# A convolution and two MLPs on one core: the weights' decode by a timetable in half positions, with its magnitude on ScalarE, raw words through GpSimd's queue, and a network's first layer a position sooner

## Chip, core and metric

The kernel runs on one core of a Trainium2 chip. Its time is device microseconds of one execution; less is better. Engines: PE = TensorE, DVE = VectorE, ACT = ScalarE, POOL = GpSimd, SP = SyncE, which here only issues DMAs. Every engine works through its own instructions in order.

## What is computed

The reference convolves `u = x * v` along the sequence with a filter that a small network makes out of position embeddings, multiplies with `x`, and sends the result through two MLPs:

```python
# x, v: (2, 12480, 128); pos_emb: (12480, 64); S = 12480
h_mlp = np.maximum(pos_emb @ w1, 0.0) @ w2
h_filt = h_mlp * np.exp(-0.01 * pos)[:, None]
u = x * v
y = irfft(rfft(u, n=2 * S) * rfft(h_filt, n=2 * S))[:, :S]
x = (x * y).reshape(24960, 128)

r = np.maximum(x @ moe_w_in, 0.0)        # w_in (128, 2048), w_out (2048, 128)
x = (r * r) @ moe_w_out
h = x @ moe2_w_in
out = (h * np.cos(h)) @ moe2_w_out
```

## The kernel before

The order of every engine's instructions is written out by hand. There are three stages.

**Stage 1** (the first `with ExitStack() as st` block) transforms the inputs over the first of two factors of the sequence length. It loops over 30 chunks of two positions each, 60 positions (`seq`). A chunk is loaded by SP into one of `LDB = 5` slots (`load`, tile `ld`; chunk q + 5 is issued when PE is done with chunk q). POOL multiplies `x` and `v` into `ut` (`times`, up to `LM = 4` positions ahead). PE makes the filter network's first layer for a whole chunk (`mlp1`, tiles `hp` and `hT`), and its second layer for a position (`prep`, tile `hp2`); ACT moves both out of PSUM. `pair` then runs four matmuls of 384 columns into `A` (in the order lists `x4`; the trace has two records for each), ACT copies a half of the results to `v`, and DVE adds and subtracts into `bt`. ACT's queue stores `bt` of a chunk to the DRAM tensor `Bs` (`store`); `bt` has `BT = 3` buffers, so a chunk's `bt` waits for the store of three chunks before.

Between positions the MLPs' weights are decoded. They come as 64-bit floats, seen as pairs of 32-bit words, and end as two float32r tensors each: `wh`, the rounded value, and `wl`, the rest. There are 16 decode steps (`WORDER`) of 128 x 512 weights. In the kernel before, `weight` is a generator with seven `yield`s per step, and `decode(2)` behind each of the positions 2 to 58 moves it on by two of them, so that a step takes 3.5 positions. SP loads the raw words (`wr`, two buffers), one step ahead.

**Stage 2** reloads `Bs` in the other order (`load2`, tile `B`), forms products with the filter's spectrum and transforms back, writing `Ds`. Its first reload waits for the store of chunk 27; `direct` and `load_late` bring the last chunks, in part straight out of `bt`.

**Stage 3** (from some 460 us on) runs the rest of the transform and both MLPs, in a fixed schedule of steps.

Of the kernel before, what the change touches and what calls it, by code (L numbers as in the profile page):

```python
# [25 lines left out]
NCH, CB = 30, 2  # L26
# [4 lines left out]
NF = DFF // 128  # L31
# [5 lines left out]
WORDER = [0, 1, 2, 3, 4, 5, 6, 7, 8, 12, 9, 13, 10, 14, 11, 15]  # L37
# [20 lines left out]
def conv_moe(ctx, tc, t):  # L58
    nc = tc.nc
# [13 lines left out]
    W = {}  # L73
# [4 lines left out]
    wt = ctx.enter_context(tc.tile_pool(name="wt", bufs=1))
    raws = {}

    def raw_of(step):
        m, f0 = divmod(step, 4)
        f = slice(4 * f0, 4 * f0 + 4)
        raw = wt.tile([128, 4, 128, 2], I32, tag="wr", name="wr", bufs=2)
        src = t[("moe_w_in", "moe_w_out", "moe2_w_in", "moe2_w_out")[m]].bitcast(I32)
        src = src.rearrange("(f p) (e t) -> p f e t" if m % 2 else "p (f e t) -> p f e t", f=NF, t=2)
        nc.sync.dma_start(out=raw, in_=src[:, f])
        raws[step] = raw, W[1 + m // 2, m % 2], f

    def weight(step):  # L90
        if step not in raws:
            raw_of(step)
        n = WORDER.index(step) + 1
        if n < 16:
            raw_of(WORDER[n])
        raw, (wh, wl), f = raws.pop(step)
        lo, hi = raw.bitcast(U32)[:, :, :, 0], raw[:, :, :, 1]
        a, b, r = (wt.tile([128, 4, 128], I32, tag=f"w_{n}", name=f"w_{n}") for n in "abr")
        af, bf, rf = a.bitcast(F32), b.bitcast(F32), r.bitcast(F32)
        ts = nc.vector.tensor_scalar  # L100
        yield
        ts(out=a, in0=hi, scalar1=0x7fffffff, scalar2=None, op0=ALU.bitwise_and)
        ts(out=b, in0=hi, scalar1=-0x80000000, scalar2=0x40000000, op0=ALU.bitwise_and, op1=ALU.bitwise_xor)
        yield
        ts(out=af, in0=af, scalar1=2.0 ** -15, scalar2=122880.0, op0=ALU.max, op1=ALU.min)
        yield
        ts(out=a, in0=a, scalar1=4, scalar2=1, op0=ALU.logical_shift_left, op1=ALU.logical_shift_right)
        nc.vector.tensor_tensor(out=a, in0=a, in1=b, op=ALU.bitwise_xor)
        yield
        ts(out=b, in0=a, scalar1=-0x800000, scalar2=None, op0=ALU.bitwise_and)  # L110
        yield
        nc.scalar.activation(wh[:, f], af, AF.Copy)
        nc.vector.scalar_tensor_tensor(out=rf, in0=lo, scalar=2.0 ** -52, in1=bf, op0=ALU.mult, op1=ALU.mult)
        yield
        nc.gpsimd.tensor_tensor(out=bf, in0=af, in1=wh[:, f].bitcast(F32), op=ALU.subtract)
        yield
        nc.gpsimd.tensor_tensor(out=wl[:, f], in0=bf, in1=rf, op=ALU.add)

    steps = (x for k in WORDER for x in weight(k))

    def decode(n):
        for _ in range(n):
            next(steps, None)
# [23 lines left out]

    with ExitStack() as st:
        out1 = st.enter_context(tc.tile_pool(name="out1", bufs=BT))
        c1 = st.enter_context(tc.tile_pool(name="c1", bufs=1))  # L150
        ring1 = st.enter_context(tc.tile_pool(name="ring1", bufs=LDB - NB, side="right"))
        io = st.enter_context(tc.tile_pool(name="io1", bufs=2))
        wk = st.enter_context(tc.tile_pool(name="wk1", bufs=2))
        psA = st.enter_context(tc.tile_pool(name="psA", bufs=3, space=PSUM))
        psM = st.enter_context(tc.tile_pool(name="psM", bufs=2, space=PSUM))

# [86 lines left out]
        def upto(kind, fn, n, end):  # L243
            while done[kind] < min(n, end):
                fn(done[kind])
                done[kind] += 1

        def last():
# [6 lines left out]
                          in_=bass.AP(t["ld"].tensor, 0, [[CB * (NCH - LATE) * 768, KE], [1, CB * (NCH - LATE) * 768]]))  # L255
        nc.scalar.dma_start(out=Gt, in_=t["G"])
        nc.scalar.dma_start(out=It, in_=t["IG"])
        for n, (q, i) in enumerate(seq):
            lead = min(LA, n + 1) if n else 1
            upto("mlp", mlp1, (n + lead - 1) // CB + 1, NCH)  # L260
            upto("times", lambda m: times(*seq[m]), n + min(LM, n + 1), len(seq))
            upto("prep", lambda m: prep(*seq[m]), n + lead, len(seq))
            pair(q, i, last if n == len(seq) - 1 else None)
            upto("mlp", mlp1, (n + lead + 1) // CB + 1 if n else 1, NCH)
            if i == 0 and q:
                if q > LATE:
                    store_late(q - 1)
                if q < NCH - 1:
                    store(q - 1)
            if (q, i) == (LATE, 0):  # L270
                load2(0)
                load2(1)
            if (q, i) == (NCH - 1, 0):
                load_late(0, CB * (NCH - 1 - LATE))
                direct(q, 0, 0)
                direct(q, 0, 1)
            if (q, i) == (NCH - 1, 1):
                load_late(1)
                load2(2)
                store(q - 1, nc.sync)  # L280
                store(q, nc.sync)
                load_late(2)
            if i == 1:
                upto("load", load, q + LDB + 1, NCH)
            if 1 < n < WS:
                decode(2)
        unread = psM.tile([128, 2 * D], F32, tag="m", name="unread")
        for _ in range(FILL[0]):
            nc.tensor.matmul(unread, w1b, w2b, start=True, stop=True)
# [515 lines left out]
```

## Time and profile before

| | |
|---|---|
| time before, median of 3 runs | 2731.67 us (2728.38 to 2733.35) |
| profiled execution, its own time | 2726.36 us |
| span of the profile (first to last instruction) | 2724.3 us |
| busy: PE, DVE, ACT, POOL | 2681.8, 2402.7, 2383.1, 1353.2 us |
| stage 1 ends (last matmul into `A`) | about 224 us |

The span is that of the profiled execution; its own time has some 2 us around it. Busy times are sums over the whole span, so they say little of stage 1, which is 8% of it; that stage is read from tables of stretches and from the rows in order of time.

### The profile page before, as it was taken

How to read it: one execution, taken by the hardware profiler on the slowest of the kernel's cores; microseconds unless marked ns; L12 is line 12 of the kernel's file. 1: busy time of each engine (PE TensorE's matmuls, PEld its weight loads, DVE VectorE, ACT ScalarE, POOL GpSimd, SP SyncE). 2: the span in 40 equal slices, each digit the busy share in tenths (PEclk: the TensorE clock that was granted, in tenths of full speed). 3: DMA queues.
4: the chain of work that ended last, by engine and by line, in shares of the span. 5: the costliest groups of instructions: out<-in, count | busy, mean ns of one | idle time of the engine just before them, and what ended most of it. 6: DMA issues, size and time to landing. Idle time of an engine off the chain costs nothing.

```text
span 2724.3 us, 38773 instructions
## 1 busy us (share of the span) xinstructions
PE 2681.8 (98%) x11762; PEld 2104.9 (77%) x11762; DVE 2402.7 (88%) x4675; ACT 2383.1 (87%) x4295; POOL 1353.2 (50%) x1050
## 2 busy tenths in 40 slices
PE   8998999999999999999999999999999999999999
PEld 5554444888888888888888888888888888888887
DVE  6997998888888888888888888888888888888888
ACT  4446997899999999999999999999999999999998
POOL 4565886244444444444444444444444444444455
PEclk9999999999999999999999999999999999999999
DMA  9997997110100110101110101111101111101000
GB/s 396 421 411 260 298 300 232 46 29 31 30 26 23 32 29 18 43 16 33 29 33 16 45 16 33 29 32 29 32 17 33 29 33 29 32 17 32 17 9 10
DMA packets 86771, 219.64 MB, mean 81 GB/s; under 512 B 6025, under 2 KB 49633, under 8 KB 82689
## 3 DMA queue, kind: packets, MB, share of 16 engines
q1 hardware_dynamic: 79298, 180.24, 20.1%
q10 hardware_dynamic: 7263, 36.92, 3.3%
q8 instruction: 93, 1.52, 0.2%
q14 instruction: 117, 0.96, 0.1%
HBM read 140.37 MB, written 77.07 MB: 80 GB/s over the span
## 4 chain that ended last, share of the span: by engine, by line
PE 81%; ACT 1%; DVE 1%; issue 0%; SPq 0%; POOLq 0%; POOL 0%; DMA 0%; DVEq 0%; ACTq 0%
PE h L565 13%; PE h L567 13%; PE y L581 13%; PE h L566 13%; PE y L579 13%; PE y L580 13%; PE pc L531 4%; DVE g L653 0%; ACT k L630 0%; DVE r L638 0%; ACT r L604 0%; DVE gh L663 0%; ACT g L610 0%; ACT c L645 0%; ACT gh L661 0%
## 5 line engine op out<-in xcount | busy, mean ns | idle before, releaser
L670 POOL TENSOR_TENSOR gl<-g,gh 128x512 fp32r<-128x512 f32 (+2 forms) x800 | 1040.8, 1301 | 1220.1 <-ACT gh L661 717.4
L653 DVE TENSOR_TENSOR g<-h,c 128x512 f32<-128x512 f32 (+2 forms) x800 | 538.6, 673 | 208.5 <-ACT c L645 197.4
L630 ACT ACTIVATE k<-h,quarter 128x512 int32<-128x512 f32 (+2 forms) x800 | 540.7, 676 | 121.5 <-PE h L567 117.4
L565 PE MATMUL h<-zh,wh 128*128 128x512 f32 (+2 forms) x1600 | 624.9, 391 | 1.2 <-DVE zh L549 0.9
L581 PE MATMUL y<-gl,wh 128*128 128x512 f32 (+2 forms) x1600 | 617.8, 386 | 4.1 <-POOL gl L670 2.2
L579 PE MATMUL y<-gh,wl 128*128 128x512 f32 (+2 forms) x1600 | 616.2, 385 | 0.7 <-DVE gh L617 0.7
L567 PE MATMUL h<-zh,wl 128*128 128x512 f32 (+2 forms) x1600 | 615.2, 384 | 0.0
L566 PE MATMUL h<-zl,wh 128*128 128x512 f32 (+2 forms) x1600 | 614.3, 384 | 0.0
L580 PE MATMUL y<-gh,wh 128*128 128x512 f32 (+2 forms) x1600 | 614.1, 384 | 0.0
L645 ACT ACTIVATE c<-r,halfpi 128x512 f32<-128x512 f32 (+2 forms) x800 | 565.4, 707 | 2.6 <-DVE r L638 2.6
L624 DVE TENSOR_TENSOR gl<-g,gh 128x512 fp32r<-128x512 f32 (+2 forms) x800 | 535.8, 670 | 1.1
L638 DVE CUSTOM_DVE_ANT_0 r<-h,k 128x512 f32<-128x512 f32 (+2 forms) x800 | 535.6, 669 | 0.0
L604 ACT ACTIVATE r<-h 128x512 f32<-128x512 f32 (+2 forms) x800 | 471.5, 589 | 69.2 <-PE h L567 57.0
L610 ACT ACTIVATE g<-r 128x512 f32<-128x512 f32 (+2 forms) x800 | 492.9, 616 | 1.0 <-DVE gl L624 0.4
L617 DVE CAST gh<-g 128x512 fp32r<-128x512 f32 (+2 forms) x800 | 331.9, 415 | 37.8 <-ACT g L610 34.9
L581 PEld LDWEIGHTS y<-gl,wh 128*128 128x128 f32 x1600 | 300.3, 188 | 70.3 <-POOL gl L670 7.7
L579 PEld LDWEIGHTS y<-gh,wl 128*128 128x128 f32 x1600 | 300.4, 188 | 61.2 <-DVE zl L592 1.2
L580 PEld LDWEIGHTS y<-gh,wh 128*128 128x128 f32 x1600 | 300.7, 188 | 59.6
L567 PEld LDWEIGHTS h<-zh,wl 128*128 128x128 f32 x1600 | 300.4, 188 | 59.7
L565 PEld LDWEIGHTS h<-zh,wh 128*128 128x128 f32 x1600 | 300.9, 188 | 56.9 <-issue 1.0
L566 PEld LDWEIGHTS h<-zl,wh 128*128 128x128 f32 x1600 | 300.7, 188 | 54.9
L661 ACT ACTIVATE gh<-g 128x512 fp32r<-128x512 f32 (+2 forms) x400 | 246.0, 615 | 0.1
(67 smaller groups left out, 2426.2 us busy)
## 6 DMA issues: line engine op xcount, KB each, us to landing
ld<-ld SPq DMA_DIRECT2D x30, 1336.0 KB
B<-Bs SPq DMA_DIRECT2D x25, 1536.0 KB
dt<-Ds SPq DMA_DIRECT2D x59, 416.0 KB
Ds<-dt SPq DMA_DIRECT2D x24, 960.0 KB
Bs<-bt ACTq DMA_DIRECT2D x28, 768.0 KB
Bs<-bt ACTq DMA_DIRECT2D x28, 480.0 KB
xt<-xT SPq DMA_DIRECT2D x60, 208.0 KB
out<-o SPq DMA_DIRECT2D x47, 256.0 KB
```

The source lines that it names most:

```text
L565: nc.tensor.matmul(h[:, :n], wh[:, f, :], zh[:, :n], start=True, stop=False)
L566: nc.tensor.matmul(h[:, :n], wh[:, f, :], zl[:, :n], start=False, stop=False)
L567: nc.tensor.matmul(h[:, :n], wl[:, f, :], zh[:, :n], start=False, stop=True)
L579: nc.tensor.matmul(y[:, :n], wl[:, f, :], gh[:, :n], start=a, stop=False)
L580: nc.tensor.matmul(y[:, :n], wh[:, f, :], gh[:, :n], start=False, stop=False)
L581: nc.tensor.matmul(y[:, :n], wh[:, f, :], gl[:, :n], start=False, stop=b)
L624: nc.vector.tensor_tensor(out=gl[:, :n], in0=g[:, :n], in1=gh[:, :n].bitcast(F32), op=ALU.subtract)
L630: nc.scalar.activation(k[:, :n], hp[2, u][:, :n], AF.Identity, scale=-1.0, bias=quarter)
L638: nc.vector._custom_dve(TENSOR_ADD_SAT, out=r[:, :n], in0=h[:, :n], in1=k[:, :n], s0=0.25, s1=-0.75)
L645: nc.scalar.activation(c[:, :n], r[:, :n], AF.Sin, bias=halfpi, scale=TWO_PI)
L653: nc.vector.tensor_tensor(out=g[:, :n], in0=h[:, :n], in1=c[:, :n], op=ALU.mult)
L670: nc.gpsimd.tensor_tensor(out=gl[:, :n], in0=g[:, :n], in1=gh[:, :n].bitcast(F32), op=ALU.subtract)
```

## The change

The decode becomes a timetable. Step k starts at half position 8 + 20 k / 3 (whole part), so a step comes every 10/3 positions, and each of its parts has a place in half positions behind that start: 0 `open_` (ACT), 2 `clamp`, 3 `shift`, 5 `exponent` and 6 `low` (DVE), 6 `high` (ACT), 9 `rest` and 10 `both` (POOL). At 8 the raw words of step k + 3 are loaded. `decode(n)` runs behind every position n and does what is planned for half positions 2n and 2n + 1.

The magnitude of the high word is taken by an ACT instruction (Abs with a scale) where two DVE instructions took magnitude and sign apart; the sign is merged back in by one instruction with two tensors, and the exponent is written over the raw word. DVE has five instructions a step instead of seven. The raw words get three buffers instead of two and are loaded through GpSimd's queue, not SP's. The decode's tiles move into stage 1's own memory. From position 9 on, `mlp1` is called a position sooner.

```diff
-WS = 59
+RAWS, PART0 = 3, 8
...
-        raw = wt.tile([128, 4, 128, 2], I32, tag="wr", name="wr", bufs=2)
-        nc.sync.dma_start(out=raw, in_=src[:, f])
-    def weight(step):
-        raw, (wh, wl), f = raws.pop(step)
-        lo, hi = raw.bitcast(U32)[:, :, :, 0], raw[:, :, :, 1]
-        yield
-        ts(out=a, in0=hi, scalar1=0x7fffffff, scalar2=None, op0=ALU.bitwise_and)
-        ts(out=b, in0=hi, scalar1=-0x80000000, scalar2=0x40000000, op0=ALU.bitwise_and, op1=ALU.bitwise_xor)
-        yield
-        ts(out=af, in0=af, scalar1=2.0 ** -15, scalar2=122880.0, op0=ALU.max, op1=ALU.min)
-        yield
-        ts(out=a, in0=a, scalar1=4, scalar2=1, op0=ALU.logical_shift_left, op1=ALU.logical_shift_right)
-        nc.vector.tensor_tensor(out=a, in0=a, in1=b, op=ALU.bitwise_xor)
-        yield
-        ts(out=b, in0=a, scalar1=-0x800000, scalar2=None, op0=ALU.bitwise_and)
-        yield
-        nc.scalar.activation(wh[:, f], af, AF.Copy)
-        nc.vector.scalar_tensor_tensor(out=rf, in0=lo, scalar=2.0 ** -52, in1=bf, op0=ALU.mult, op1=ALU.mult)
-        yield
-        nc.gpsimd.tensor_tensor(out=bf, in0=af, in1=wh[:, f].bitcast(F32), op=ALU.subtract)
-        yield
-        nc.gpsimd.tensor_tensor(out=wl[:, f], in0=bf, in1=rf, op=ALU.add)
...
+            raw = wt.tile([128, 4, 128, 2], I32, tag="wr", name="wr", bufs=RAWS)
+            nc.gpsimd.dma_start(out=raw, in_=src[:, f])
...
+        def weight(k):
+            at, step = PART0 + k * 20 // 3, WORDER[k]
+            def open_():
+                nc.scalar.activation(a[0].bitcast(F32), hold[0].bitcast(F32)[:, :, :, 1], AF.Abs, scale=2.0 ** 16)
+            def clamp():
+                nc.vector.tensor_scalar(out=af, in0=af, scalar1=2.0, scalar2=1.875 * 2.0 ** 32, op0=ALU.max, op1=ALU.min)
+            def shift():
+                nc.vector.tensor_scalar(out=a[0], in0=a[0], scalar1=3, scalar2=None, op0=ALU.logical_shift_left)
+                nc.vector.scalar_tensor_tensor(out=a[0], in0=hold[0][:, :, :, 1], scalar=-0x80000000, in1=a[0],
+                                               op0=ALU.bitwise_and, op1=ALU.bitwise_or)
+            def exponent():
+                nc.vector.tensor_scalar(out=hold[0][:, :, :, 1], in0=a[0], scalar1=-0x800000, scalar2=None, op0=ALU.bitwise_and)
+            def high():
+                nc.scalar.activation(hold[1][0][:, hold[2]], a[0].bitcast(F32), AF.Copy)
+            def low():
+                nc.vector.scalar_tensor_tensor(out=r[0], in0=raw.bitcast(U32)[:, :, :, 0], scalar=2.0 ** -52,
+                                               in1=raw.bitcast(F32)[:, :, :, 1], op0=ALU.mult, op1=ALU.mult)
+            def rest():
+                nc.gpsimd.tensor_tensor(out=af, in0=af, in1=hold[1][0][:, hold[2]].bitcast(F32), op=ALU.subtract)
+            def both():
+                nc.gpsimd.tensor_tensor(out=hold[1][1][:, hold[2]], in0=a[0].bitcast(F32), in1=r[0], op=ALU.add)
+            for d, fn in ((0, open_), (2, clamp), (3, shift), (5, exponent), (6, low), (6, high), (9, rest), (10, both)):
+                plan(d, fn)
+            if k + RAWS < len(WORDER):
+                plan(8, lambda: raw_of(WORDER[k + RAWS]))
...
+        def decode(n):
+            if n == 1:
+                for k in range(RAWS):
+                    raw_of(WORDER[k])
+            for h in (2 * n, 2 * n + 1):
+                for fn in planned.pop(h, ()):
+                    fn()
...
-            upto("mlp", mlp1, (n + lead + 1) // CB + 1 if n else 1, NCH)
+            upto("mlp", mlp1, (n + lead + 1 + (n > 8)) // CB + 1 if n else 1, NCH)
...
-            if 1 < n < WS:
-                decode(2)
+            decode(n)
```

In the order of instructions this shows at three places. First DVE, early in stage 1; `bt x2` are the two of one position, `w_a`, `w_b` and `w_r` the decode's tiles, `wr` the raw words. Before, one step:

```order
L102 TENSOR_SCALAR w_a<-wr 128x512
L103 TENSOR_SCALAR w_b<-wr 128x512
L216 TENSOR_TENSOR bt<-A,v 128x2x384 x2
L105 TENSOR_SCALAR w_a<-w_a 128x512
L107 TENSOR_SCALAR w_a<-w_a 128x512
L108 TENSOR_TENSOR w_a<-w_a,w_b 128x512
L216 TENSOR_TENSOR bt<-A,v 128x2x384 x2
L110 TENSOR_SCALAR w_b<-w_a 128x512
L113 SCALAR_TENSOR_TENSOR w_r<-wr,w_b 128x512
```

and of the change:

```order
L135 TENSOR_SCALAR w_a<-w_a 128x512
L138 TENSOR_SCALAR w_a<-w_a 128x512
L139 SCALAR_TENSOR_TENSOR w_a<-wr,w_a 128x512
L239 TENSOR_TENSOR bt<-A,v 128x2x384 x2
L143 TENSOR_SCALAR wr<-w_a 128x512
L239 TENSOR_TENSOR bt<-A,v 128x2x384 x2
L151 SCALAR_TENSOR_TENSOR w_r<-wr 128x512
```

Two instructions on the raw words left DVE, and what remains stands between the same `bt` pairs.

Second POOL, where a decode step's last two parts stand among the products `ut`. Before:

```order
L191 TENSOR_TENSOR ut<-ld 104x2x256 x3
L115 TENSOR_TENSOR w_b<-w_a,wh_67 128x512
L191 TENSOR_TENSOR ut<-ld 104x2x256
L117 TENSOR_TENSOR wl_68<-w_b,w_r 128x512
L191 TENSOR_TENSOR ut<-ld 104x2x256 x3
```

and of the change:

```order
L115 DMA wr<-moe_w_out 128x4x256
L156 TENSOR_TENSOR w_a<-w_a,wh_67 128x512
L214 TENSOR_TENSOR ut<-ld 104x2x256
L159 TENSOR_TENSOR wl_68<-w_a,w_r 128x512
L214 TENSOR_TENSOR ut<-ld 104x2x256 x2
```

A DMA issue for the raw words now stands ahead of each step's `rest` on POOL; on SP, where they stood between the loads of chunks, there are none left.

Third PE, at the ninth and tenth position; `hp` out of `ld` is the network's first layer for a chunk, `hp` out of `hT` its second for a position, `A x4` a position's matmuls. Before:

```order
L182 MATMUL hp<-ld,first 128x208
L196 MATMUL hp_373<-first,hT 104x256
L212 MATMUL A<-ut,ld 128x384 x4
L196 MATMUL hp_395<-first,hT 104x256
L212 MATMUL A<-ut,ld 128x384 x4
L182 MATMUL hp<-ld,first 128x208
L196 MATMUL hp_419<-first,hT 104x256
L212 MATMUL A<-ut,ld 128x384 x4
```

and of the change:

```order
L205 MATMUL hp<-ld,first 128x208
L219 MATMUL hp_359<-first,hT 104x256
L235 MATMUL A<-ut,ld 128x384 x4
L205 MATMUL hp<-ld,first 128x208
L219 MATMUL hp_387<-first,hT 104x256
L235 MATMUL A<-ut,ld 128x384 x4
L219 MATMUL hp_408<-first,hT 104x256
L235 MATMUL A<-ut,ld 128x384 x4
```

From here on the first layer stands ahead of a chunk's second position instead of the next chunk's first.

## Rows read from the trace of the kernel before

**Rows 1.** The page: DMA busy share in 40 slices of the span.

```profile
DMA  9997997110100110101110101111101111101000
```

**Rows 2.** Stretches A:B and length in us; busy us by engine (instructions); clock; DMA share; GB/s.

```profile
10.00:20.00 10.00, 9.06 (x21) 4.69 (x20) 1.82 (x2) 3.10 (x9) 5.19 (x5) 1.00 1.01 414
40.00:200.00 160.00, 149.64 (x503) 91.28 (x502) 156.83 (x182) 77.13 (x173) 89.99 (x70) 1.00 1.02 418
200.00:218.00 18.00, 15.97 (x54) 9.66 (x53) 17.40 (x24) 8.37 (x19) 9.64 (x8) 1.00 0.67 243
```

**Rows 3.** Groups by shape, 10 to 224 us: busy us, mean ns | idle before.

```profile
L216 DVE TENSOR_TENSOR bt<-A,v 128x768 f32<-128x768 f32 x118 | 107.1, 948 | 24.3 <-PE A L212 21.8 <-ACT v L214 1.5 <-issue 0.8
...
L102 DVE TENSOR_SCALAR w_a<-wr 128x512 int32<-128x512 int32 x16 | 23.1, 1442 | 0.5 <-DMA wr<-moe_w_in 0.5
L103 DVE TENSOR_SCALAR w_b<-wr 128x512 int32<-128x512 int32 x16 | 21.7, 1358 | 0.0
...
L105 DVE TENSOR_SCALAR w_a<-w_a 128x512 f32<-128x512 f32 x16 | 17.1, 1067 | 0.0
...
L108 DVE TENSOR_TENSOR w_a<-w_a,w_b 128x512 int32<-128x512 int32 x16 | 11.1, 692 | 0.6
L113 DVE SCALAR_TENSOR_TENSOR w_r<-wr,w_b 128x512 f32<-128x512 uint32 x16 | 11.0, 687 | 0.3
L112 ACT ACTIVATE wh<-w_a 128x512 fp32r<-128x512 f32 x16 | 10.1, 631 | 36.4 <-DVE w_a L108 36.4
...
L110 DVE TENSOR_SCALAR w_b<-w_a 128x512 int32<-128x512 int32 x16 | 6.7, 422 | 0.3
L107 DVE TENSOR_SCALAR w_a<-w_a 128x512 int32<-128x512 int32 x16 | 6.7, 419 | 0.3
```

**Rows 4.** DVE in order of time: start, us, what it is, count.

```profile
52.43 1.81 DVE L216 TENSOR_TENSOR bt<-A,v 128x768 f32<-128x768 f32 x2
```

**Rows 5.** DMA issues, 0 to 230 us: queue, count, KB (1024 bytes) each.

```profile
ld<-ld SPq DMA_DIRECT2D x30, 1336.0 KB
Bs<-bt ACTq DMA_DIRECT2D x28, 768.0 KB
Bs<-bt ACTq DMA_DIRECT2D x28, 480.0 KB
...
wr<-moe_w_in SPq DMA_DIRECT2D x8, 512.0 KB
```

**Rows 6.** PE in order of time: first A of chunks 1, 5, 26, 29; last A.

```profile
21.81 2.75 PE L212 MATMUL A<-ut,ld 104*128 104x384 f32 x8
...
47.34 2.75 PE L212 MATMUL A<-ut,ld 104*128 104x384 f32 x8
...
196.04 2.82 PE L212 MATMUL A<-ut,ld 104*128 104x384 f32 x8 [0.17 <-DVE bt L216]
...
217.42 4.88 PE L212 MATMUL A<-ut,ld 104*128 104x384 f32 x14
223.07 0.91 PE L212 MATMUL A<-ut,ld 104*128 104x384 f32 x2 [0.77 <-DVE bt L216]
```

**Rows 7.** Waits, 10 to 224 us: us in total, times, longest us.

```profile
PE A L212 <- DVE bt L216: 6.2, 11, 1.3
...
POOL ut L191 <- DMA ld<-ld: 2.5, 2, 1.4
...
DVE w_a L102 <- DMA wr<-moe_w_in: 0.5, 1, 0.5
```

**Rows 8.** Line L103 in stage 1: duration in ns, min/median/max.

```profile
L103 DVE TENSOR_SCALAR w_b<-wr x16: 415/1490/1500, 27.3 to 212.9; 128x512 int32<-128x512 int32 x16
```

**Rows 9.** SP's issues in order of time, 160 to 232 us.

```profile
188.78 0.33 SPq L165 DMA_DIRECT2D ld<-ld  x1
...
217.07 1.29 SPq L137 DMA_DIRECT2D B<-Bs  x2
```

**Rows 10.** DMA queues, 196 to 200 us, SP's (q1): packets, MB, share of engines.

```profile
q1 hardware_dynamic: 230, 0.50, 33.0%
```

More of the change, by code (lines that the diff above doesn't have):

```diff
@@ L76, in conv_moe @@
             W[layer, k] = tuple(cst.tile([128, NF, 128], F32R, name=f"w{p}{layer}{k}") for p in "hl")
[L78 to L83, printed above, removed]
-        raw = wt.tile([128, 4, 128, 2], I32, tag="wr", name="wr", bufs=2)
-        src = t[("moe_w_in", "moe_w_out", "moe2_w_in", "moe2_w_out")[m]].bitcast(I32)
-        src = src.rearrange("(f p) (e t) -> p f e t" if m % 2 else "p (f e t) -> p f e t", f=NF, t=2)
-        nc.sync.dma_start(out=raw, in_=src[:, f])
-        raws[step] = raw, W[1 + m // 2, m % 2], f
-    def weight(step):
[L91 to L95, printed above, removed]
-        raw, (wh, wl), f = raws.pop(step)
-        lo, hi = raw.bitcast(U32)[:, :, :, 0], raw[:, :, :, 1]
-        a, b, r = (wt.tile([128, 4, 128], I32, tag=f"w_{n}", name=f"w_{n}") for n in "abr")
-        af, bf, rf = a.bitcast(F32), b.bitcast(F32), r.bitcast(F32)
-        ts = nc.vector.tensor_scalar
-        yield
-        ts(out=a, in0=hi, scalar1=0x7fffffff, scalar2=None, op0=ALU.bitwise_and)
-        ts(out=b, in0=hi, scalar1=-0x80000000, scalar2=0x40000000, op0=ALU.bitwise_and, op1=ALU.bitwise_xor)
-        yield
-        ts(out=af, in0=af, scalar1=2.0 ** -15, scalar2=122880.0, op0=ALU.max, op1=ALU.min)
-        yield
-        ts(out=a, in0=a, scalar1=4, scalar2=1, op0=ALU.logical_shift_left, op1=ALU.logical_shift_right)
-        nc.vector.tensor_tensor(out=a, in0=a, in1=b, op=ALU.bitwise_xor)
-        yield
-        ts(out=b, in0=a, scalar1=-0x800000, scalar2=None, op0=ALU.bitwise_and)
-        yield
-        nc.scalar.activation(wh[:, f], af, AF.Copy)
-        nc.vector.scalar_tensor_tensor(out=rf, in0=lo, scalar=2.0 ** -52, in1=bf, op0=ALU.mult, op1=ALU.mult)
-        yield
-        nc.gpsimd.tensor_tensor(out=bf, in0=af, in1=wh[:, f].bitcast(F32), op=ALU.subtract)
-        yield
-        nc.gpsimd.tensor_tensor(out=wl[:, f], in0=bf, in1=rf, op=ALU.add)
[L119 to L123, printed above, removed]
     conv_st = ExitStack()
@@ L149, in conv_moe @@
         out1 = st.enter_context(tc.tile_pool(name="out1", bufs=BT))
+        wt = st.enter_context(tc.tile_pool(name="wt", bufs=1))
         c1 = st.enter_context(tc.tile_pool(name="c1", bufs=1))
@@ L153, in conv_moe, with raw_of @@
         wk = st.enter_context(tc.tile_pool(name="wk1", bufs=2))
+        raws = {}
+        def raw_of(step):
+            m, f0 = divmod(step, 4)
+            f = slice(4 * f0, 4 * f0 + 4)
+            raw = wt.tile([128, 4, 128, 2], I32, tag="wr", name="wr", bufs=RAWS)
+            src = t[("moe_w_in", "moe_w_out", "moe2_w_in", "moe2_w_out")[m]].bitcast(I32)
+            src = src.rearrange("(f p) (e t) -> p f e t" if m % 2 else "p (f e t) -> p f e t", f=NF, t=2)
+            nc.gpsimd.dma_start(out=raw, in_=src[:, f])
+            raws[step] = raw, W[1 + m // 2, m % 2], f
@@ new lines, in conv_moe, with plan @@
+        planned = {}
+        def weight(k):
+            at, step = PART0 + k * 20 // 3, WORDER[k]
+            a, r, hold = [], [], []
+            def plan(d, *fns):
+                planned.setdefault(at + d, []).extend(fns)
+            def open_():
+                hold.extend(raws.pop(step))
+                a.append(wt.tile([128, 4, 128], I32, tag="w_a", name="w_a", bufs=2))
+                nc.scalar.activation(a[0].bitcast(F32), hold[0].bitcast(F32)[:, :, :, 1], AF.Abs, scale=2.0 ** 16)
+            def clamp():
+                af = a[0].bitcast(F32)
+                nc.vector.tensor_scalar(out=af, in0=af, scalar1=2.0, scalar2=1.875 * 2.0 ** 32, op0=ALU.max, op1=ALU.min)
[8 more added lines that the diff above has]
+            def low():
+                raw = hold[0]
+                r.append(wt.tile([128, 4, 128], F32, tag="w_r", name="w_r"))
+                nc.vector.scalar_tensor_tensor(out=r[0], in0=raw.bitcast(U32)[:, :, :, 0], scalar=2.0 ** -52,
+                                               in1=raw.bitcast(F32)[:, :, :, 1], op0=ALU.mult, op1=ALU.mult)
+            def rest():
+                af = a[0].bitcast(F32)
+                nc.gpsimd.tensor_tensor(out=af, in0=af, in1=hold[1][0][:, hold[2]].bitcast(F32), op=ALU.subtract)
[5 more added lines that the diff above has]
+                plan(8, lambda: raw_of(WORDER[k + RAWS]))
@@ L154, in conv_moe @@
+        for k in range(len(WORDER)):
+            weight(k)
+        def decode(n):
[5 more added lines that the diff above has]
+                    fn()
         psA = st.enter_context(tc.tile_pool(name="psA", bufs=3, space=PSUM))
```

## Prediction

> **What bounds the kernel now.** I read the page first: of its 40 DMA slices (68 us each) only the first seven are busy, to 477 us [rows 1]. Behind them lies a dense stream of matmuls that this change doesn't touch. The edited code runs in stage 1, the first 224 us, and a microsecond gained there is one at the end as long as the two stages behind it merely start sooner.
>
> So next the table of stretches. From 40 to 200 us DVE is busy 156.83 us of 160, which looks like the bound. But the same row has a DMA share of 1.02 at 418 GB/s, and between 10 and 20 us, when five loads stand queued and little else runs, the share is 1.01 at 414 GB/s [rows 2]: 418 is all that these transfers get. Two resources are full at once. What each allows per chunk (two positions) can be worked out.
>
> DVE: a decode step takes 1442 + 1358 + 1067 + 419 + 692 + 422 + 687 = 6087 ns [rows 3], and comes every 3.5 positions (seven yields, two per position), which is 3.48 us per chunk. The two bt instructions of a position take 1.81 us back to back [rows 4], a little under twice their mean of 948 ns [rows 3], since they overlap; two positions add 3.62. Sum 7.10 us.
>
> Transfers: a chunk loads 1336 KB and stores 768 + 480 KB; a decode step loads 512 KB per 1.75 chunks, 293 KB [rows 5]. 2877 KB are 2.946 MB, at 418 GB/s **7.05 us**.
>
> PE: before the first decode instructions reach DVE, four chunks go from 21.81 to 47.34 us, **6.38 us** each. After that 24 chunks go from 47.34 to 217.42, 7.09 each [rows 6]. So the pace is DVE's 7.10, with the transfers' 7.05 right under it, and PE's 6.38 far below. That nearly equal second floor is what this prediction turns on.
>
> The list of waits agrees: PE's wait for DVE before A is 6.2 us in all, and nothing waits long for a load (POOL 2.5 us, DVE 0.5 us) [rows 7]. The buffers hide the transfers as long as they keep pace.
>
> **The change, part by part.**
>
> *DVE.* Five instructions take the place of seven. The sign, shift and mask parts have near twins in the old step: clamp as L105 (1067), shift as L107 (419), the two-tensor OR as L108 (692), exponent as L110 (422), low as L113 (687): 3287 ns [rows 3]. Sixteen steps fall from 97.4 to 52.6 us, **44.8 us off DVE**. Bounds: a single-source instruction takes 415 ns alone and 1.5 us when it meets a POOL instruction [rows 8], so the step lies between 2.6 us (none held up) and 5.9 (all three held up). I take 3.3, since the old order's shift and exponent met no POOL work while its first three did. With a step every 10/3 positions DVE then needs 3.62 + 3.29 × 2 / 3.33 = 5.6 us per chunk. At the upper bound it would be 7.2, and nothing would be won.
>
> *ACT.* Abs is 16 more instructions, taken as the old Copy, 631 ns [rows 3]: 10.1 us. ACT is busy for 77 of 160 us [rows 2], so idle time holds it. In exchange the Copy no longer sits at ACT's head waiting for DVE's XOR. If that cover were gone it would cost those 10 us.
>
> *POOL and SP.* Sixteen raw loads leave SP's queue, where an issue costs 0.33 us [rows 9]. SP only waits between loads, so this frees nothing: the load of chunk q+5 is issued when PE is done with chunk q. On POOL an issue isn't in the trace. From below it is SP's 0.33 us; from above POOL, busy for 90 of 160 us [rows 2], has 70 us idle, over 4 us per issue. Inside that it is hidden, the more so as times runs four positions ahead. Behind a late issue stand rest, both and the next times on POOL. The transferred bytes are the same, so the transfer floor stays; with a step every 1.67 chunks it is 7.08 us.
>
> *The first layer a position sooner.* PE's first-layer matmul for chunk c stood before the first position of chunk c − 1; it now stands before the second one of chunk c − 2. The work is the same; ACT's hT gets more room, but PE, which runs in order, wants the load a position (3.2 us) earlier.
>
> **The sum.** DVE's floor falls to 5.6, PE's is 6.38, so the transfers at 7.05 to 7.08 set the pace as long as loads arrive. Up to 200 us next to nothing can be gained: PE may creep nearer to the loads, not outrun them. What is left is the tail. The last load is issued at 188.78 us [rows 9]; SP's queue moves only 0.50 MB from 196 to 200 us [rows 10], part of it raw words, so the load has landed at about 200. From then until 218 us the DMA share is 0.67 [rows 2], and the stage ends at 223.98 (223.07 + 0.91) [rows 6].
>
> Lower bound: PE is no nearer to the loads than now. Chunk 26 starts at 196.04; four chunks at 6.38 end at 221.6, **2.4 us sooner**. Upper bound: all idle transfer time of the tail is used, 18 × (1 − 0.67 / 1.02) = **6.2 us**, after which the first reload of Bs (issued at 217.07 now [rows 9]) can't come sooner still. The new order sets a limit close to that: after the last hp five positions of 3.19 us remain, so with the load at 200 to 202 the end lies at 216.5 to 218.5. Against the upper end speaks that the last raw load, 512 KB or 1.25 us, moves from the idle tail into the full stretch (three steps are now fetched ahead), and that each chunk that PE draws nearer to the loads puts a store (1.28 MB, 3.1 us) ahead of the last load. I take the middle, **4 us**. Stage 2 starts on the reload, the last stores and the last bt, which all move along.
>
> The profiled execution took 2726.36 us (span 2724.3 and 2.1 around it) and would take 2722.4; the median of the runs shown is 2731.67, 5.3 higher, so I predict 2731.7 − 4 = **2727.7 us**. A measurement of this kernel can tell about 0.2%, 5.5 us, from no change; 4 us is inside that.
>
> **Rivals.**
>
> *Tail and rate both give, 5.5 to 9 us.* The full 6.2 us come back, or a fuller queue moves 1% more in 160 us (1.6 us). That the share of 1.02 lies over the 1.01 of the early queue speaks for it, that the two rates are within 1% of each other against. About 2724.5.
>
> *PE's pace.* If the transfers followed, 24 chunks would save 0.71 us each, 17 us: 2714.7. It needs 2.96 MB in 6.38 us, 464 GB/s, 11% over anything in [rows 2].
>
> *Hidden altogether.* What the tail gains is lost again on the way into stage 2, or DVE's instructions are held up by POOL more than I take. 2731.
>
> *Slower: raw words late through POOL.* ACT's Abs now takes the wait for them, in order, with v and so bt and PE's A buffers behind it. The load for step k+3 is issued at half position 8 of step k and read at 20: six positions, 19 to 21 us, against a step time of 3.5 × 3.54 = 12.4 us within which it arrives today nearly always (0.5 us of waits [rows 7]). It decides once POOL's issue plus landing takes over 19 us; each microsecond beyond costs up to 16: 2731.7 − 4 + 16 = 2743.7. What speaks for it: DVE and POOL do lock each other out, 415 ns against 1.5 us in [rows 8]. The Trainium skill (SBUF — State Buffer, "SBUF: two separate sides") goes further: descriptors of a DMA from GpSimd's queue are written by GpSimd, which a two-port DVE instruction keeps from the port, so such a transfer seems blocked, and it advises SP's or ACT's queue. By that rule a raw load would be held for some 0.4 us at each of three such instructions per step, 1.3 us, far from the 7 us of slack, so the sum would stay; no run here shows a DMA from POOL yet.
>
> **Chances.** The transfer floor with 2.4 to 5.4 us: 0.50. Tail and rate: 0.22. PE's pace: 0.08. Hidden: 0.11. Slower: 0.09. Faster by over 0.2% is the second and third, 0.30; within, the first and fourth, 0.61; slower 0.09. The range leaves out PE's pace and the slower case: 2722 to 2734.
>
> **What would show it.** In the changed profile: DVE's busy time from 40 to 200 us near 120 to 130 us; five decode instructions of 3.3 us in sum; DMA share still 1.0 up to some 200 us at about 418 GB/s, and no lower GB/s for the raw words; PE waiting for loads (hp or ut after ld) or DVE's bt waiting for stores, which it doesn't now; a tail of 6.4 us per chunk; the first reload of Bs at about 213. Wrong would be: a pace under 7.0 us before 200 us (then 418 GB/s is no floor), POOL's DMA rows of over 4 us, or ACT idle before Abs on the raw words.

## The result, and the profile after

The changed kernel takes 2748.83 us (median of 6 runs, 2743.54 to 2751.42), the kernel before 2732.49 (6 runs beside it): ratio 1.006, 95% interval 1.0047 to 1.0073. The change costs 16.3 us, where 4 us of gain were predicted. The profiled execution of the changed kernel took 2751.42 us, the slowest of its six, that of the kernel before 2726.36; so the traces are compared by stage 1, not by their spans.

TensorE (PE) in order of time, the changed kernel: first A of chunks 5 and 29, last A.

```profile
46.54 2.75 PE L235 MATMUL A<-ut,ld 104*128 104x384 f32 x8
...
236.99 4.88 PE L235 MATMUL A<-ut,ld 104*128 104x384 f32 x14
242.63 0.91 PE L235 MATMUL A<-ut,ld 104*128 104x384 f32 x2 [0.76 <-DVE bt L239]
```

24 chunks take 190.45 us, 7.94 each, where they took 7.09 [rows 6]. The stage ends at 243.54 us instead of 223.98: 19.6 us of loss in the stage that was edited. The two spans differ by 25.3 us; the other 5.7 us are no more than executions of one kernel lie apart (2728.38 to 2735.28 before). The decode step, instructions by line and form, 0 to 260 us (busy us, mean ns, then idle time before):

```profile
L135 DVE TENSOR_SCALAR w_a<-w_a 128x512 f32<-128x512 f32 x16 | 46.9, 2931 | 0.0
L139 DVE SCALAR_TENSOR_TENSOR w_a<-wr,w_a 128x512 int32<-128x512 int32 x16 | 14.9, 929 | 0.6
L151 DVE SCALAR_TENSOR_TENSOR w_r<-wr 128x512 f32<-128x512 uint32 x16 | 10.9, 682 | 0.5
L138 DVE TENSOR_SCALAR w_a<-w_a 128x512 int32<-128x512 int32 x16 | 10.5, 659 | 0.4
L143 DVE TENSOR_SCALAR wr<-w_a 128x512 int32<-128x512 int32 x16 | 6.7, 416 | 0.0
L115 POOL DMA_DIRECT2D wr<-moe_w_out x8 | 6.4, 802 | 45.0 <-DVE w_r L151 45.0
L115 POOL DMA_DIRECT2D wr<-moe_w_in x8 | 4.7, 591 | 31.0 <-DVE w_r L151 31.0
```

Exponent and low (L143, L151) are as sized. The clamp (L135) takes 2931 ns instead of 1067 [rows 3], and that is a mean over two kinds: its shortest takes 418 ns, its longest 5443. GpSimd (POOL) stands 76 us at the raw loads (45.0 + 31.0), waiting for low. One of these places in order of time:

```profile
82.54 0.79 POOL L115 DMA_DIRECT2D wr<-moe_w_out  x1 [5.24 <-DVE w_r L151]
83.35 1.28 POOL L156 TENSOR_TENSOR w_a<-w_a,wh 128x512 f32<-128x512 f32 x1
84.57 1.28 POOL L214 TENSOR_TENSOR ut<-ld 104x512 f32<-104x512 f32 x1
85.80 1.27 POOL L159 TENSOR_TENSOR wl<-w_a,w_r 128x512 fp32r<-128x512 f32 x1
86.07 3.73 DVE L135 TENSOR_SCALAR w_a<-w_a 128x512 f32<-128x512 f32 x1
87.02 2.49 POOL L214 TENSOR_TENSOR ut<-ld 104x512 f32<-104x512 f32 x2
...
90.91 1.82 DVE L239 TENSOR_TENSOR bt<-A,v 128x768 f32<-128x768 f32 x2
...
94.89 0.63 ACT L146 ACTIVATE wh<-w_a 128x512 fp32r<-128x512 f32 x1 [3.53 <-DVE bt L239]
...
96.68 4.51 PE L235 MATMUL A<-ut,ld 104*128 104x384 f32 x8 [1.91 <-ACT ut L221]
```

GpSimd waits 5.24 us, issues the load and then runs five instructions without a pause, to 89.51. The clamp starts in the midst of them and ends at 89.80. Nine of the sixteen clamps meet such a run, and each ends 0.28 to 0.30 us behind its last instruction. Behind it come a late bt, a late Copy on ACT (which waited 3.53 us for DVE), the ut copies behind that, and a PE that idles 1.91 us. Its next eight matmuls take 4.51 us instead of 2.75. The windows say why, 80 to 84 us behind an earlier stop, 96 to 100 behind this one (us; busy time and count of PE, PEld, DVE, ACT, POOL; granted clock; DMA share; GB/s):

```profile
80.00:84.00 4.00, 4.00 (x8) 2.08 (x8) 2.24 (x3) 0.81 (x1) 1.44 (x2) 0.59 1.02 419
...
96.00:100.00 4.00, 3.32 (x6) 1.92 (x7) 2.69 (x3) 2.41 (x7) 3.98 (x4) 0.62 0.87 339
...
40.00:200.00 160.00, 141.93 (x444) 85.56 (x443) 141.31 (x141) 76.90 (x169) 89.67 (x76) 0.94 0.99 376
200.00:220.00 20.00, 17.47 (x49) 10.00 (x48) 16.86 (x17) 7.88 (x17) 11.64 (x10) 0.83 0.84 338
```

In each microsecond from 97 to 100 the granted clock is 0.50, the lower of PE's two levels (1.2 of 2.4 GHz); before, it was 1.00 all through [rows 2]. Of the seven longest stops from 40 us on (1.57 to 2.79 us) five were followed by such a fall; the longest was not:

```profile
64.48 2.82 PE L235 MATMUL A<-ut,ld 104*128 104x384 f32 x8 [2.79 <-DVE bt L239]
...
79.72 4.51 PE L235 MATMUL A<-ut,ld 104*128 104x384 f32 x8 [1.87 <-ACT ut L221]
```

What the clock costs and what the waits cost can be told apart by PE's matmuls into A, the same 472 in both kernels (busy us, mean ns, then idle time before; first before, then after):

```profile
L212 PE MATMUL A<-ut,ld 104*128 104x384 f32 x472 | 166.8, 496 | 9.9 <-DVE bt L216 6.2 <-ACT v L214 2.9 <-ACT ut L198 0.8
```

```profile
L235 PE MATMUL A<-ut,ld 104*128 104x384 f32 x472 | 177.5, 520 | 22.2 <-DVE bt L239 13.2 <-ACT ut L221 6.8 <-issue 1.3
```

The same matmuls take 10.7 us longer, and PE stands still 12.3 us longer before them; before its second-layer matmuls it stands still 4.1 us less. With all its matmuls counted, PE is busy 157.69 us of the 170.08 from chunk 5 to 29 before, and 169.85 of 190.45 after: 12.2 us by the clock (0.93 in the mean of this stretch, instead of 1.00) and 8.2 us by waits, together the 20.4 us by which this stretch grew. The DMA share is still 0.99, but only 376 GB/s move, and past the start of the stage hardly anything waits for a transfer (DVE's bt 2.1 us in all).

### The profile page after: what moved, and what is told of

It reads as the page before. It is cut to its first block, busy times and chain, and to the rows that moved or that the text cites. A ratio compares the mean times of both kernels' runs of the same rounds, so it can differ in the third digit from the quotient of the medians.

```text
span 2749.6 us, 38811 instructions
## 1 busy us (share of the span) xinstructions
PE 2695.7 (98%) x11762; PEld 2112.3 (77%) x11762; DVE 2399.0 (87%) x4643; ACT 2391.3 (87%) x4311; POOL 1360.8 (49%) x1066
## 4 chain that ended last, share of the span: by engine, by line
PE 80%; ACT 1%; DVE 1%; DMA 0%; issue 0%; SPq 0%; POOLq 0%; DVEq 0%
PE h L587 13%; PE h L589 13%; PE h L588 13%; PE y L603 13%; PE y L601 13%; PE y L602 13%; PE pc L553 4%; DVE g L675 0%; ACT k L652 0%; DVE r L660 0%; DMA dt<-Ds 0%; ACT c L667 0%; DVE gh L685 0%; DMA Ds<-dt 0%; ACT r L626 0%
```

## The experiments

The first theory (held up): GpSimd's wait makes a run of instructions, the run holds the clamp, PE stops, its clock falls. Rivals: transfers from GpSimd's queue are slower (2.946 MB at 370 GB/s is just the pace seen), or the sooner first layer costs. Each ratio is to the kernel before, measured beside the run; its medians lie between 2730.64 and 2732.49 us, so times of different experiments can be set against each other to some 2 us only.

**1. Raw loads on SP again.**

```diff
-            nc.gpsimd.dma_start(out=raw, in_=src[:, f])
+            nc.sync.dma_start(out=raw, in_=src[:, f])
```

> Edit: the changed kernel with the raw loads issued by SP again, the rest as changed. Held-up theory (GpSimd stands at the raw load's head until low has read the buffer, then runs its queued work without a pause, DVE's clamp is held for all of it, bt comes late, TensorE idles and its granted clock falls): GpSimd waits for low no more, clamp falls from a mean of 2.9 us to 1.0-2.0, the granted clock of stage 1 stays over 0.95, time 2728 to 2738 us. Queue theory (transfers issued by GpSimd move slower, 2.946 MB at some 370 GB/s is 7.96 us a chunk, which is the pace seen): back to 418 GB/s and 7.05 us a chunk, 2728 us. First-layer theory (the sooner matmul is to blame): stays at 2749.

2735.02 us, ratio 1.001 (1.000 to 1.002); clamp 837 ns, still less than foretold. 13 us of the 16 are in this line. The held-up theory's range holds; the queue theory foretold 2728, 7 us less.

**2. First layer as before.**

```diff
-            upto("mlp", mlp1, (n + lead + 1 + (n > 8)) // CB + 1 if n else 1, NCH)
+            upto("mlp", mlp1, (n + lead + 1) // CB + 1 if n else 1, NCH)
```

> Edit: the changed kernel with the network's first layer at its old place, the rest as changed. Held-up and queue theories: 2746 to 2752 us, clamp still 2.9 us, the granted clock still falls to 0.5-0.7 in places. First-layer theory: 2728 to 2735 us.

2746.79, 1.0057 (1.0046 to 1.0069); clamp 3128 ns. The first layer is not what the 16 us are; the 2 us between 2748.83 and 2746.79 can't be told from nothing here.

**3. Raw load later on GpSimd's queue.**

```diff
-                plan(8, lambda: raw_of(WORDER[k + RAWS]))
+                plan(12, lambda: raw_of(WORDER[k + RAWS]))
```

> Edit: the changed kernel with each raw load planned at half position 12 of its step instead of 8, still on GpSimd's queue and four positions ahead of its use. Held-up theory: low is done by then, so GpSimd's wait for it falls from 76 us in all to under 15, the bursts get shorter, clamp falls below 2 us, 2730 to 2741 us. Queue theory: the rate stays at some 370 GB/s and the pace at 7.9 us a chunk, 2746 to 2752 us. First-layer theory: 2746 to 2752.

2736.44, 1.0021 (1.0012 to 1.003). GpSimd doesn't wait at the load any more, clamp 1375 ns, and from 40 to 120 us all queues together move 416 to 423 GB/s (403 and 356 in the changed kernel), with the raw words still on GpSimd's queue. The queue theory, which wanted 2746 to 2752 us, falls.

**4. Clamp with two tensor sources.**

```diff
-                nc.vector.tensor_scalar(out=af, in0=af, scalar1=2.0, scalar2=1.875 * 2.0 ** 32, op0=ALU.max, op1=ALU.min)
+                nc.vector.scalar_tensor_tensor(out=af, in0=af, scalar=2.0, in1=lim[:, None, :].to_broadcast([128, 4, 128]),
+                                               op0=ALU.max, op1=ALU.min)
```

> Edit: the changed kernel with the clamp written with two tensor sources (its upper limit from a small constant tile) instead of one, the same arithmetic. The two-source instructions of the step were held up little (0.68 and 0.93 us). Held-up theory: clamp takes 0.7 to 1.0 us instead of 2.9 although GpSimd still waits for low and still runs in bursts, bt is no longer late, granted clock over 0.95, 2728 to 2738 us. Queue theory: the pace stays at 7.9 us a chunk, 2746 to 2752. First-layer theory: 2746 to 2752.

2750.36, 1.0072 (1.006 to 1.0084); the clamp takes 3379 ns. My premise was wrong: an instruction with two sources in SBUF is held just as long, up to 5.7 us. The two-source instructions of the step had not met such a run; they were not immune to it. Against the held-up theory itself this says nothing.

**5. The wait alone** (same place and queue; only the step that is loaded differs).

```diff
-            if k + RAWS < len(WORDER):
-                plan(8, lambda: raw_of(WORDER[k + RAWS]))
+            if k and k + RAWS - 1 < len(WORDER):
+                plan(8, lambda: raw_of(WORDER[k + RAWS - 1]))
```

> Edit: the changed kernel with the raw load at the same place of GpSimd's queue (half position 8 of step k), but for step k+2 instead of k+3, into the buffer whose last reader, low of step k-1, is long done. So only GpSimd's wait goes; order, queue and bytes stay. Held-up theory: the wait of 76 us in all falls under 10, clamp falls below 2 us on average, the time falls by 9 to 15 us to 2734 to 2740. If the later place in the queue was what helped when the load stood at half position 12, nothing comes: 2746 to 2752 us.

2736.73, 1.0022 (1.0012 to 1.0031). GpSimd's wait at the load is gone, clamp 826 ns: 10 to 12 us of the 16 (10 by the ratios).

**6. Both: SP, and later.**

```diff
-            nc.gpsimd.dma_start(out=raw, in_=src[:, f])
+            nc.sync.dma_start(out=raw, in_=src[:, f])
...
-                plan(8, lambda: raw_of(WORDER[k + RAWS]))
+                plan(12, lambda: raw_of(WORDER[k + RAWS]))
```

> Edit: the changed kernel with the raw loads issued by SP and planned at half position 12, so that neither GpSimd nor SP waits for low ahead of other work. Floor theory (with the held-up DVE gone the transfers at 418 GB/s set the pace of 7.05 us a chunk, and a tail of some 4 us is won, as predicted): 2724 to 2730 us, granted clock 1.0. Clock theory (a stage that waits on transfers leaves TensorE idle for some us now and then, its granted clock falls, and that gives the gain back): 2731 to 2737 us, with stretches at 0.6 to 0.95 in stage 1.

2736.06, 1.0019 (1.0011 to 1.0028), with a granted clock of 0.94 from 40 to 200 us: no gain as the floor theory wanted it; the clock theory's range holds. ACT's Abs now waits 12.5 us for raw words.

**7 and 8. The two small parts, alone, in the kernel before**: its raw loads through GpSimd (line as in 1, the other way), and its first layer sooner (as in 2, the other way).

> Edit: the kernel before with its raw loads issued through GpSimd's queue, nothing else. There the load for the next step is asked for when a step begins, into the buffer of the step before, whose reader is done. Held-up theory: GpSimd waits little at it, 2729 to 2736 us. Queue theory (transfers issued by GpSimd are slower or slow the others): 2740 to 2752 us.

> Edit: the kernel before with the network's first layer a position sooner, nothing else. Held-up theory: no change that can be told, 2728 to 2735 us. If the sooner first layer costs by itself (TensorE, in order, wants a load a position earlier): 2736 to 2742 us.

The sooner first layer: 2733.06, 1.0007 (0.9998 to 1.0016), nothing that can be told. The raw loads through GpSimd alone: **2754.20, 1.0088 (1.0074 to 1.0102)**, more than the whole change, although GpSimd never waits at them. That contradicts the first theory, which needed the wait; the queue theory, refuted by experiment 3, comes nearer with its 2740 to 2752. Its order of time:

```profile
79.56 0.80 POOL L87 DMA_DIRECT2D wr<-moe_w_out  x1
80.38 3.72 POOL L191 TENSOR_TENSOR ut<-ld 104x512 f32<-104x512 f32 x3
...
79.83 4.56 DVE L103 TENSOR_SCALAR w_b<-wr 128x512 int32<-128x512 int32 x1
```

In the kernel before, the same three ut products let this DVE instruction in after at most one of them (1.50 us [rows 8]). Here a DMA stands ahead of them, and it waits for all three; so do six others of the sixteen (4.36 to 4.58 us). So a second theory (port): a DMA that GpSimd issues keeps DVE out until GpSimd's run ends; the wait in the changed kernel only makes the run long. (The port is an inference; the runs show how long DVE is held.) Two runs set it against the first.

**9. The wait and the run, without the DMA in it.**

```diff
-            nc.gpsimd.dma_start(out=raw, in_=src[:, f])
+            nc.sync.dma_start(out=raw, in_=src[:, f])
...
-            if k + RAWS < len(WORDER):
-                plan(8, lambda: raw_of(WORDER[k + RAWS]))
+            plan(8, lambda: nc.gpsimd.tensor_copy(seen, r[0][:, 0, 0:1]))
+            if k + RAWS < len(WORDER):
+                plan(12, lambda: raw_of(WORDER[k + RAWS]))
```

> Edit: the changed kernel with the raw loads on SP (asked for at half position 12), and in their old place on GpSimd's queue a copy of one column of low's result, 128 numbers. So GpSimd still waits for low in that place and then runs its queued work without a pause, but no DMA of its own stands in that run. Port theory (a DMA that GpSimd issues keeps DVE's instructions on SBUF out until GpSimd's run of instructions ends; without one DVE gets in after at most one of them): clamp is 1.7 us at most and 0.7 to 1.1 on average, 2732 to 2740 us. Run theory (any run of GpSimd's behind a wait holds DVE to its end): clamp up to 4 or 5 us, over 2.3 on average, 2745 to 2752 us.

2734.71, 1.0015 (1.0005 to 1.0025). GpSimd still waits 77.0 us for low and still runs on without a pause, but DVE gets in:

```profile
54.63 0.19 POOL L164 COPY seen<-w_r 128x1 f32<-128x1 f32 x1 [5.01 <-DVE w_r L152]
54.77 1.27 POOL L157 TENSOR_TENSOR w_a<-w_a,wh 128x512 f32<-128x512 f32 x1
56.00 1.28 POOL L216 TENSOR_TENSOR ut<-ld 104x512 f32<-104x512 f32 x1
57.24 1.27 POOL L160 TENSOR_TENSOR wl<-w_a,w_r 128x512 fp32r<-128x512 f32 x1
58.47 2.69 POOL L216 TENSOR_TENSOR ut<-ld 104x512 f32<-104x512 f32 x2
...
57.00 1.79 DVE L136 TENSOR_SCALAR w_a<-w_a 128x512 f32<-128x512 f32 x1
```

The clamp of 57.00 sits through the rest of one GpSimd instruction and the whole of the next and ends at 58.79, with two more of the run still to come (to 61.16). Its mean is 1076 ns, as foretold; its longest, 1.88 us, is over the 1.7 that the port theory allowed. Five fences follow, one line's instructions in each (count, then ns as min/median/max): the clamp of the changed kernel and of experiment 9, then the second mask instruction of the kernel before with raw loads through GpSimd and of experiment 10, and last the first mask instruction of the kernel before.

```profile
L135 DVE TENSOR_SCALAR w_a<-w_a x16: 418/3807/5443, 35.0 to 232.5; 128x512 f32<-128x512 f32 x16
```

```profile
L136 DVE TENSOR_SCALAR w_a<-w_a x16: 415/1104/1877, 35.7 to 217.8; 128x512 f32<-128x512 f32 x16
```

```profile
L103 DVE TENSOR_SCALAR w_b<-wr x16: 408/422/4576, 26.5 to 239.3; 128x512 int32<-128x512 int32 x16
```

```profile
L102 DVE TENSOR_SCALAR w_b<-wr x16: 415/1489/1496, 26.1 to 218.9; 128x512 int32<-128x512 int32 x16
```

```profile
L102 DVE TENSOR_SCALAR w_a<-wr x16: 417/1043/2536, 27.0 to 212.6; 128x512 int32<-128x512 int32 x16
```

The last shows that one GpSimd instruction is not the most without a DMA. In the kernel before, the first mask instruction takes 2.53 to 2.54 us seven times: the rest of a ut product and the whole of the wl behind it. That is the longest hold there, and experiment 10 keeps it (2.54); the holds to the end of a longer run are the DMA's.

The changed kernel has a test of this of its own. Four of its runs have the DMA at their head but then a pause of 0.07 to 0.08 us, here between 71.89 and 71.97:

```profile
70.61 1.28 POOL L156 TENSOR_TENSOR w_a<-w_a,wh 128x512 f32<-128x512 f32 x1
71.97 1.28 POOL L159 TENSOR_TENSOR wl<-w_a,w_r 128x512 fp32r<-128x512 f32 x1
73.20 4.10 POOL L214 TENSOR_TENSOR ut<-ld 104x512 f32<-104x512 f32 x3
73.60 1.16 DVE L135 TENSOR_SCALAR w_a<-w_a 128x512 f32<-128x512 f32 x1
```

The clamps behind the pause take 0.52 to 1.16 us, although three more GpSimd instructions follow.

**10. The kernel before, raw loads through GpSimd, but at the end of its run** (a third buffer; the pool moves into stage 1).

```diff
-        nc.sync.dma_start(out=raw, in_=src[:, f])
+        nc.gpsimd.dma_start(out=raw, in_=src[:, f])
...
-        if n < 16:
-            raw_of(WORDER[n])
+        if n == 1:
+            raw_of(WORDER[1])
...
         yield
+        if n + 1 < 16:
+            raw_of(WORDER[n + 1])
         nc.gpsimd.tensor_tensor(out=bf, in0=af, in1=wh[:, f].bitcast(F32), op=ALU.subtract)
```

> Edit: the kernel before with its raw loads through GpSimd's queue, but asked for right ahead of rest, which waits for low (a third buffer, so that no load waits). There the DMA is the last of a run of GpSimd's and an idle time follows; in the run with the raw loads on GpSimd at the start of a step it stood at the head of one. Port theory: the second mask instruction is 1.7 us at most again (4.58 there), 2729 to 2737 us. Queue theory (transfers issued by GpSimd cost by themselves): 2748 to 2756 us.

2734.23, 1.0013 (1.0003 to 1.0023): with the same queue and the same bytes 20 us come back, and the second mask instruction's longest is 1496 ns. The port theory holds in both, but for its bound of one instruction; run and queue theory fall.

**11 and 12. What do the transfers bound?** Raw loads left out but for the first buffers, in experiment 6's kernel and in the kernel before:

```diff
+            if len(kept) == RAWS:
+                raws[step] = kept[WORDER.index(step) % RAWS], W[1 + m // 2, m % 2], f
+                return
             raw = wt.tile([128, 4, 128, 2], I32, tag="wr", name="wr", bufs=RAWS)
+            kept.append(raw)
```

> Edit: the changed kernel with raw loads on SP, but only the first three of sixteen; the other thirteen steps decode what stands in the three buffers, so the weights are not the real ones; all else is done. Transfers fall from 2.94 to 2.64 MB a chunk, 6.3 us at 418 GB/s, and DVE needs 5.6 to 6.0. Floor theory (transfers bound the stage once DVE is relieved): the pace falls to TensorE's 6.4 us a chunk, 2712 to 2719 us. If something else holds the stage (order, hand-over between engines, clock): 2728 us or more.

> Edit: the kernel before, but only the first two of sixteen raw loads; the other steps decode what stands in the two buffers, so the weights are not the real ones; all else is done. By the prediction's two floors (DVE 7.10 us a chunk, transfers 7.05) DVE's stays: 2727 to 2733 us. If the transfers had set the pace before: 2712 to 2722 us.

2724.99, 0.9976 (0.9964 to 0.9989), and 2729.39, 1.000 (0.999 to 1.0009). Windows of the two:

```profile
40.00:200.00 160.00, 153.09 (x514) 94.81 (x513) 135.59 (x161) 86.52 (x190) 100.42 (x75) 0.99 0.99 388
```

```profile
40.00:200.00 160.00, 148.73 (x498) 90.23 (x497) 155.79 (x181) 75.68 (x171) 90.01 (x70) 1.00 0.98 372
```

The kernel before loses nothing and gains nothing with a tenth fewer bytes: DVE set its pace. Its DMA share stays 0.98 although only 372 GB/s move, so a share near 1 doesn't say that the transfers are full. And with both DVE and the transfers relieved, the mended kernel stands 5.7 us under the kernel before, not the 17 of PE's pace: 6.86 us a chunk instead of 6.38, and a time between the two ranges that were foretold.

Against experiment 6, which has the raw loads and is otherwise the same, it is 11 us faster, and stage 1 ends at 217.90 us instead of 232.72. So once DVE is relieved the raw words' transfers do cost, by their bytes or by when they come; these runs don't part the two.

**13 and 14. Where the last microseconds went.** To experiment 5's kernel: work for DVE that nobody reads, and the first layer as before.

```diff
+                if not between and q > 4:
+                    nc.vector.tensor_tensor(out=v[:, 0], in0=A[0][:, 0, 0:384], in1=v[:, 0], op=ALU.add)
```

> Edit: the kernel of the run in which only GpSimd's wait was taken away, and on DVE after each position's two bt instructions (from chunk 5 on) one more of half their width, whose result nobody reads. It reads PSUM and v, and takes about 0.55 us by the rows of that form. DVE then needs some 6.9 us a chunk instead of 5.8. Pacing theory (a stage that can run ahead of its transfers runs until its buffers are used up, stops for some us at a time, and TensorE's granted clock falls at each stop; a DVE just slower than the transfers' 7.05 us spreads the stops out): fewer stretches under a granted clock of 1.0, and 2729 to 2734 us, faster than the 2736.7 without the added work. Work theory (added work on a busy engine only costs): 2737 to 2745 us.

> Edit: the kernel of the run in which only GpSimd's wait was taken away, with the network's first layer at its old place as well; of the parts of the change that the runs so far put a cost on, none is left but the relieved DVE itself. First-layer part costs something: 2730 to 2734 us. Costs nothing: 2735 to 2738 us.

2739.40, 1.0025 (1.0016 to 1.0034), and 2734.69, 1.0014 (1.0006 to 1.0023). The added work brings nothing: the pacing theory isn't borne out. It isn't cleanly tested either, since the added instruction reads A, and PE waits 15.0 us (9 times) for it. The first layer's place costs at most the 2 us between 2736.73 and 2734.69, inside the spread of the runs; 2734.69 lies between the two ranges that were foretold.

What the mended kernels show instead of a gain, experiment 5 in order of time:

```profile
80.87 1.82 DVE L239 TENSOR_TENSOR bt<-A,v 128x768 f32<-128x768 f32 x2 [4.19 <-DMA Bs<-bt]
82.84 4.51 PE L235 MATMUL A<-ut,ld 104*128 104x384 f32 x8 [2.92 <-DVE bt L239]
...
222.91 4.88 PE L235 MATMUL A<-ut,ld 104*128 104x384 f32 x14
```

its waits (us in total, times, longest) and its windows:

```profile
DVE bt L239 <- DMA Bs<-bt: 24.1, 10, 4.3
```

```profile
40.00:80.00 40.00, 38.97 (x133) 24.15 (x132) 32.82 (x38) 23.22 (x52) 29.29 (x24) 1.00 1.01 422
80.00:120.00 40.00, 35.02 (x108) 21.72 (x109) 27.83 (x36) 18.31 (x41) 22.49 (x19) 0.91 1.01 401
```

and experiment 9, in which ACT's Abs stands at a raw word that SP brought late, with v behind it:

```profile
79.03 0.67 ACT L132 ACTIVATE w_a<-wr 128x512 f32<-128x512 f32 x1 [4.67 <-DMA wr<-moe_w_out]
...
80.78 4.44 PE L237 MATMUL A<-ut,ld 104*128 104x384 f32 x8
```

PE runs at its own pace until the three bt buffers are all on their way out (or a raw word is late), stops for 2 to 3 us, and in both places shown then gets a lower clock: 4.4 to 4.5 us for a group of 2.75. (At 197.24 us of experiment 5 a stop of 3.04 us was followed by a group at full speed, 2.82.) Experiment 5's chunk 29 begins at 222.91 us, 5.5 later than before [rows 6].

## Why the prediction was wrong, by its steps

**The step that failed: DVE's 3287 ns, and the bound on a held instruction.** I took 1.5 us as the most that a meeting with GpSimd costs, from one line of the kernel before [rows 8], whose runs have no DMA in them. Even there it was too low: the line ahead of it took up to 2.54 us. The step took 5617 ns (2931 + 929 + 682 + 659 + 416), still under my upper bound of 5.9, where I had written that nothing would be won. But a mean says little: DVE then needs 3.62 + 5.62 × 2 / 3.33 = 7.0 us per chunk, less than before, and the pace was 7.94. What costs is single holds of 3.7 to 5.4 us, behind which bt and the ut copies come late and PE stops. Experiments 9 and 10 show their cause, the DMA in GpSimd's run; runs without it, or without the wait that makes the run long, give back 10 to 14 of the 16 us (2748.83 against 2734.7 to 2736.7). That wait had no price in the prediction either: with three buffers the load for step k + 3 goes into step k's, and GpSimd stood 76 us at it for low.

**A term that was missing: PE's clock.** The sum had no price for a PE that stops. In the changed kernel the lower granted clock takes 12.2 us of the 20.4 lost between chunks 5 and 29, more than the 8.2 us of waits that bring it on.

**The slower rival** had the right sign by another way. It priced raw words that come late to ACT's Abs. In the changed kernel ACT never waits for them (in experiments 6 and 9, with the loads on SP and later, 12.5 and 14.1 us), and POOL's DMA rows take 0.59 and 0.80 us, far below the 4 us that I named; the pace didn't fall under 7.0 either, so none of my three signs of being wrong came up. The lock between DVE and POOL, which I named in its favour, was the point, but I priced it as a delay of the transfer only. The Trainium skill (SBUF — State Buffer, "SBUF: two separate sides") says of the pair of ports that whichever of the two engines starts first has it for the whole instruction, and counts DVE instructions with two SBUF inputs among those that need it. Experiment 4 (two inputs, held) agrees. If every GpSimd instruction were a new chance for DVE, a hold would end with the one that is running; the traces differ, by a little without a DMA (2.54 us, the rest of one and the whole of the next) and by much behind a DMA of GpSimd's, with holds of 3.7 to 5.4 us to the end of the run. The Trainium skill's advice there, for a DMA that starves behind DVE, is to use SP's or ACT's queue. Here DVE was the one that waited, and the advice held by 13.8 us (2748.83 to 2735.02).

**The transfers' floor** was read too boldly. That the share of 1.02 means full was refuted by experiment 12 (0.98 at 372 GB/s); DVE as the pace of the kernel before was right. What the transfers allow at most stays open: from 40 to 200 us no run moved more than 418 GB/s, and without the raw words' bytes experiment 11 is 11 us faster than 6. The relieved kernels move 398 to 410 GB/s from 40 to 200 us in experiments 6 and 9, not 418.

**The tail's 4 us** never showed. (Five positions of 3.19 us behind a load at 200 to 202 us end at 216 to 218, not at 216.5 to 218.5; nothing hangs on that.) The mended kernels (1, 3, 5, 6, 9, 14) stand at 2734.7 to 2736.7, 3 to 6 us above before. Their stops show where time goes, and experiment 11 what brings most of them: without the raw loads stage 1 ends 14.8 us sooner than in experiment 6. Whether these transfers cost by their bytes, by late raw words (12.5 us of waits in experiment 6) or by late stores (24.1 us in experiment 5, 10.7 in 11), stays open. **The first layer** was taken to cost nothing. Three comparisons each put it at some 2 us (2748.83 and 2746.79, 2733.06 and 2730.64, 2736.73 and 2734.69), each within its noise; so a small cost is neither shown nor excluded.

## What to carry to other kernels

Before a DMA is moved to GpSimd's queue, look at what GpSimd runs behind it without a pause, and which DVE instructions on SBUF fall into that time: put the DMA last in a run, or on another queue. Price a wait on the way to TensorE by what it does to the granted clock too, not by its length alone. And read a DMA share together with the GB/s: it was 0.98 here at 372 and 1.02 at 418.

## What was not expected of the hardware

A DMA issued by GpSimd took 0.59 us (8 of them) and 0.80 us (the other 8) of that engine. If further GpSimd instructions followed without a pause, a DVE instruction on SBUF that came in their midst ended some 0.3 us after the last of them (89.51 and 89.80; 84.10 and 84.39), with two sources some 0.55 us (90.40 and 90.96 in experiment 4). Behind a pause of 0.07 to 0.08 us in such a run the clamps took 0.52 to 1.16 us, and without the DMA no hold was longer than 2.54 us. The bt instructions, which read PSUM and v, were never held (948 ns mean before, 949 after). A stop of PE of 1.91 us was followed by a granted clock of 0.50 from 97 to 100 us; one of 2.79 us, at 64.48, by none below 1.00.
